# ScalarE's order in the second product's steps, the end of the routing, eight weight loads from another queue, and a branch made short

## The chip, the cores and the metric

The kernel runs on one core of one Trainium2 chip, as one program. The engines of the core run their own instruction streams and meet at semaphores: TensorE (PE in the profile, its weight loads PEld), VectorE (DVE), ScalarE (ACT), GpSimd (POOL) and SyncE (SP, which here only issues DMAs). The metric is the device time of one execution in microseconds. Three runs of the kernel before took 572.85, 573.92 and 575.16 us, median 573.92.

## The reference

Three parts follow each other, on 1536 tokens of width 512:

```python
# attention, 2 x 8 heads, 768 positions, head size 64
keep = is_global | is_local              # 8 global keys, 96 local ones
scores = np.where(keep, scale * q @ k.T - slope * dist, -1e9)
x = softmax(scores) @ v
# gated product
xn = x / rms(x) * rms_g
x = (silu(xn @ w_gate) * (xn @ w_val)) @ w_out        # d_ff 1536
# top-1 mixture of 8 experts; tokens with a skip score <= 0 are passed on
do = x @ w_skip > 0
e = argmax(x[do] @ w_gate_moe)           # 8 logits
y = prob[e] * (relu(x[do] @ w1[e]) @ w2[e])           # 512 -> 1024 -> 512
out = x;  out[do] = x[do] + y
```

## The kernel before

Numbers of full precision are needed, so each large matrix product is done as three: every operand is cast to a high part (names with h: `wh`, `hh`, `ewh`, `exh`) by ACT, and the rest (`wl`, `hl`, `ewl`, `exl`) is a subtraction on DVE or POOL. The order of the instructions on each engine is the order in which the code is written (a manual schedule), so a hook inside a loop places work by hand. Each engine works its own list off in order.

- **Start.** SP issues the loads; DVE works out a flag (are the attention's two limits in the range that the fast code handles?). `with tc.If(flag == 0): general_attention(s)` (L962) holds a general attention, which these inputs don't take: every engine branches over it. Its six query blocks are written out, inside a loop over head pairs.
- **Banded attention**, 24 items: scores (L222), maximum (L233), exponential (L244), product with v.
- **First product** `gemm1` (L517): gate and value, results `h` kept in SBUF, 18 tiles.
- **Second product** `gemm2(t)` (L583), twelve steps, one for 128 tokens each: 36 matmuls `px` of 128x512, ACT scales them out as `x2` (L587), a DMA of it goes to `out` from ACT's queue (L590) and another to a copy `xm` from SP's. Inside the loop over the twelve blocks k of a step stand hooks: `turn(t-1)` behind k=1 transposes the last step's x2 (L559, `pxt`) and ACT copies it to `x2t` (L560); `logits(t-1)` and `route(t-1)` behind k=4 compute the router's logits (L568, `lg`), on DVE the choice of an expert, and `exps` on ACT the exponential (`rex`, L656); `slots` behind k=9. Ahead of a step stand `ranks(t-2)` (L678/L679, `rk`): counts of tokens by expert. Behind a step, `split_h(t+2)` casts the operand of a later step in six pieces (ACT `hh` L546, DVE `hl` L547), and in the steps 1, 2, 5 and 6 `split_next` casts 3, 2, 2 and 1 tiles of the experts' weights (ACT `ewh` L824, DVE `ewl` L833, 128x1024 each).
- **Routing's end.** Each expert takes 128 token slots. Expert 0's tokens aren't gathered from DRAM but built on PE in `x0` by products with a selection matrix (`add`, L1180), for the last three steps by hand: `choose` makes the matrix from the rank `rk0` of the last tokens. While expert 0's first product runs, a hook `gathers` works out the token indices (`ids`, `gi_s`) and POOL gathers the tokens of experts 1, 0, 2, 3 by indirect DMAs (L848).
- **Experts** 0 to 8 (the ninth takes what didn't fit): `tx` transposes and splits the tokens (L858, L861), `up` (L871, `eph`), `relu`, `th` transposes and splits again (L890 to L893), `down` (L903, `epy`), `put` (L911 `eo`, and an indirect DMA to `out` from POOL, L913). Weight tiles of 512 KB come by 72 loads from SP (L816) into a ring of tiles (`eraw`), each split by ACT and DVE into two more tiles; a load waits until a tile is free, and its place in SP's list is where `load_next` is called.

Of the kernel before, what the change touches and what calls it, by code (L numbers as in the profile page):

```python
# [113 lines left out]
def general_attention(s):  # L114

    nc, tc = s.nc, s.tc
    with tc.tile_pool(name="ga", bufs=1) as p, tc.tile_pool(name="gap", bufs=1, space=PSUM) as ps:
        slopes = p.tile([128, 8, 2], F32, name="gslopes")
        for j in range(16):
            nc.gpsimd.memset(slopes[:, j // 2, j % 2:j % 2 + 1], -(2.0 ** -(j % 8 + 1)))  # L120
        with tc.For_i(0, 8, 1) as pr:
            slope = p.tile([128, 2], F32, name="gslope")
            nc.vector.tensor_copy(slope, slopes[:, ds(pr, 1), :].rearrange("p a b -> p (a b)"))
            for hh in range(2):
                r = slice(64 * hh, 64 * hh + 64)
                q = p.tile([64, 768], F32, name="gq")
                nc.sync.dma_start(q.rearrange("p (a i c) -> p a i c", a=1, c=64),
                                  s.qx.rearrange("a p (i c) -> p a i c", c=128)[r, ds(pr, 1), :, r])
                k = p.tile([64, 928], F32, name="gk")
                nc.sync.dma_start(k.rearrange("p (a n) -> p a n", a=1),  # L130
                                  s.kx.rearrange("a p n -> p a n")[r, ds(pr, 1), :])
                v = p.tile([128, 11, 64], F32, name="gv")
                nc.sync.dma_start(v.rearrange("p (a b) d -> p a b d", a=1),
                                  s.vx.rearrange("a p h b d -> p a h b d")[:, ds(pr, 1), hh])
                nc.vector.tensor_scalar(q, q, 0.125, None, ALU.mult)
                xo = p.tile([64, 768], F32, name="gxo")
                for i in range(6):
                    rel = p.tile([128, 768], F32, name="grel")
                    nc.gpsimd.iota(rel, pattern=[[-1, 768]], base=128 * i, channel_multiplier=1,
                                   allow_small_or_imprecise_dtypes=True)  # L140
                    key = p.tile([128, 768], F32, name="gkey")
                    nc.gpsimd.iota(key, pattern=[[1, 768]], base=0, channel_multiplier=0,
                                   allow_small_or_imprecise_dtypes=True)
                    loc = p.tile([128, 768], F32, name="gloc")
                    dist, keep = distance(s, rel, key, loc)
                    sc = ps.tile([128, 6, 128], F32, name="gsc")
                    for j in range(6):
                        nc.tensor.matmul(sc[:, j, :], lhsT=q[:, 128 * i:128 * i + 128],
                                         rhs=k[:, 160 * j:160 * j + 128], start=True, stop=True)
                    t = p.tile([128, 768], F32, name="gt")  # L150
                    nc.vector.scalar_tensor_tensor(
                        out=t, in0=dist, scalar=slope[:, hh:hh + 1], in1=sc.rearrange("p a b -> p (a b)"),
                        op0=ALU.mult, op1=ALU.add)
                    nc.vector.tensor_tensor(t, t, keep, ALU.mult)
                    nc.vector.tensor_scalar(keep, keep, 1.0, -NEG, ALU.subtract, ALU.mult)
                    nc.vector.tensor_tensor(t, t, keep, ALU.add)
                    m = p.tile([128, 1], F32, name="gm")
                    nc.vector.tensor_reduce(m, t, AX.X, ALU.max)
                    nc.vector.tensor_scalar(t, t, m, None, ALU.subtract)
                    z = p.tile([128, 1], F32, name="gz")  # L160
                    nc.scalar.activation(t, t, AF.Exp, accum_out=z)
                    nc.vector.tensor_scalar(z, z, 1e-9, None, ALU.add)
                    nc.vector.reciprocal(z, z)
                    nc.vector.tensor_scalar(t, t, z, None, ALU.mult)
                    pt = ps.tile([128, 6, 128], F32, name="gpt")
                    for j in range(6):
                        nc.tensor.transpose(pt[:, j, :], t[:, 128 * j:128 * j + 128], s.ident)
                    pts = loc.rearrange("p (a b) -> p a b", a=6)
                    nc.vector.tensor_copy(pts, pt)
                    po = ps.tile([64, 128], F32, name="gpo")  # L170
                    for j in range(6):
                        nc.tensor.matmul(po, lhsT=v[:, 2 * j, :], rhs=pts[:, j, :],
                                         start=j == 0, stop=j == 5)
                    nc.vector.tensor_copy(xo[:, 128 * i:128 * i + 128], po)
# [451 lines left out]

def route(s, t):

    V, p = s.nc.vector, s.hpool
# [169 lines left out]
class Expert:  # L799
# [52 lines left out]

    def tx(self, xt=None):
        s, nc = self.s, self.s.nc
        if xt is None:
            xt = s.ps_e.tile([128, 4, 128], F32, name="ext", bufs=1)
            for k in range(4):
                nc.tensor.transpose(xt[:, k, :], self.xg[:, 128 * k:128 * k + 128], s.ident)  # L858
        self.xh = s.epool.tile([128, 4, 128], F32R, name="exh", bufs=2)
        self.xl = s.epool.tile([128, 4, 128], F32R, name="exl", bufs=2)  # L860
        nc.scalar.copy(self.xh, xt)  # L861
        nc.vector.tensor_tensor(self.xl, xt, f(self.xh), ALU.subtract)

    def up(self, hook=None):
# [54 lines left out]
def attn_moe_kernel(ctx, tc, qx, kx, vx, rel, ints, wgv, w_out, rms_g, w9, w9t, w1, w2, out):  # L919
# [216 lines left out]
    def routed(t):  # L1136
        logits(s, t)
        run(route(s, t))
        exps(s, t)

    for t in range(11):
        if t >= 2:
            ranks(s, t - 2)
            run(select(s, t - 2))
        if t >= 2:
            run(gates(s, t - 2))
        gemm2(s, t, {
            (0, 1): lambda: t >= 1 and turn(s, t - 1),
            (0, 4): lambda: t >= 1 and routed(t - 1),
            (0, 9): lambda: t >= 2 and slots(s, t - 2)})  # L1150
        if t + 2 < 12:
            split_h(s, t + 2)
        if t in (1, 5, 9):
            for q in range(6):
                s.slots.add(early if t < 9 and q == 0 else big, [f"h{t // 4}{q}"])
        split_next({1: 3, 2: 2, 5: 2, 6: 1}.get(t, 0))
        load_next({6: 4, 9: 5}.get(t, 0))


    slt = s.ixpool.tile([24, 256], F32, name="slt", bufs=1)  # L1160
# [36 lines left out]
    def tenth():  # L1197
        ranks(s, 10)
        choose(10, s.rk[10], s.oh[:, 10, 0:1])

    def adds():
        add(s.x2[9], first[9], start=True)
        add(s.early, s.ident)
        free_wo(0, 3)
        load_next(4)

    gemm2(s, 11, {
        (0, 2): lambda: turn(s, 10), (0, 5): early, (0, 9): lambda: routed(10),
        (256, 4): lambda: turn(s, 11, 0), (256, 6): tenth, (256, 10): adds})
    logits(s, 11, range(2))  # L1210
    add(s.x2[10], first[10])
    turn(s, 11, 1)
    logits(s, 11, range(2, 4))
    lg = s.lg[11]
    nc.scalar.dma_start(s.out[1408:1536, :], s.x2[11])
    rest = route(s, 11)
# [4 lines left out]
                                   op0=ALU.is_equal, op1=ALU.mult)  # L1221
    rk0 = s.ps_g.tile([128, 1], F32, name="rk0", tag="ps0", bufs=2)
    nc.tensor.matmul(rk0, lhsT=s.ones16, rhs=s.cum[:, 11, 0:1], start=True, stop=False)
    nc.tensor.matmul(rk0, lhsT=s.tri, rhs=oh0, start=False, stop=True)
    choose(11, rk0, oh0)
    run(rest)
    exps(s, 11)
    add(s.x2[11], first[11], stop=True)
    free_wo(3, 6)
    ranks(s, 11, s.ps_m, "misc")  # L1230
    psr.close()
    hctx.close()
    gctx.close()
# [3 lines left out]
    s.slots.add(s.epool, ["raw8"])  # L1237
    s.ps_e = pool(phase3, "ps_e", space=PSUM)
    experts[0].tx(x0)
    run(select(s, 10), select(s, 11))  # L1240

    def gathers():
        p = ids(s.ps_m, "misc", False)
# [6 lines left out]
        for e in (1, 0, 2, 3):  # L1250
            experts[e].gather()

    experts[0].up(gathers)
    run(gates(s, 10), gates(s, 11))
    experts[0].relu()
    for t in range(9, 12):
        slots(s, t)
    slt2 = s.ixpool.tile([24, 256], F32, name="slt2", bufs=1)
    nc.vector.tensor_tensor(slt2, slt, s.sl, ALU.add)
    experts[1].tx()  # L1260
    experts[0].th()
    tab = s.ps_m.tile([128, 2, 24], F32, name="tab", tag="misc", bufs=1)
    for b in range(2):
        nc.tensor.transpose(tab[:, b, :], slt2[:, 128 * b:128 * b + 128], s.ident[0:24, 0:24])
# [125 lines left out]
```

## Time and profile before

| | us |
|---|---|
| median of three runs | 573.92 |
| the profiled execution | 574.41 |
| its span | 572.7 |
| attention | about 12 to 105 |
| first product | 105 to 310 |
| second product's steps | 310 to 439 |
| routing's end, to expert 0's first matmul | 439 to 445 |
| experts | 445 to 566 |

PE is busy 93% of the span, DVE 70%, ACT 48%, POOL 24%. In the second product the step's length is read from one rank product (`rk`) to the next; a timeline row gives start, duration, engine, line, operation, and in brackets the idle time of that engine before it with what ended it. [...]

### The profile page before, as it was taken

Reading aid. Unit: us, or ns where it says so; the run is one execution under the profiler, and the core shown is the slowest. Engines: PE = TensorE matmul, PEld = TensorE weight load, DVE = VectorE, ACT = ScalarE, POOL = GpSimd, SP = SyncE. Lnnn points to the kernel's source line nnn. Section 1 sums busy time; section 2 is a strip of 40 time slices with the busy share of each in tenths; the row PEclk is TensorE's granted clock in tenths of the full one; section 3 lists DMA queues with packets and bytes.
Section 4 is the critical chain, followed back from the end, with each engine's and each line's share of the span. In section 5 each row is a group of like instructions: output and inputs, shape, how many; then the busy total and the mean of one; then the engine's idle time right before and its main releaser. Section 6 shows DMA issues by size and latency. Waiting matters only on the chain. (4 is left out here: it accounts for less than half of the span.)

```text
span 572.7 us, 8709 instructions
## 1 busy us (share of the span) xinstructions
PE 532.6 (93%) x2932; PEld 444.9 (78%) x2932; DVE 401.0 (70%) x1014; ACT 277.7 (48%) x630; POOL 135.0 (24%) x132
## 2 busy tenths in 40 slices
PE   1899998899999999999999988989998799999994
PEld 1788887788888888888888867867888587878883
DVE  2888989557888688768864255545442299999971
ACT  0689889224323333323323444335231196988850
POOL 1445556011222222222212000000000201566201
PEclk9899999899999999999999988999999899999998
DMA  8645521021223323333206211106066899999000
GB/s 300 263 180 223 196 89 39 1 75 61 96 102 110 111 80 105 110 112 110 102 10 224 106 41 66 42 37 221 37 251 220 266 340 330 367 396 367 32 15 17
DMA packets 29511, 83.79 MB, mean 146 GB/s; under 512 B 3512, under 2 KB 3640, under 8 KB 29457
## 3 DMA queue, kind: packets, MB, share of 16 engines
q1 hardware_dynamic: 26064, 75.95, 36.7%
q0 software_dynamic: 1520, 4.03, 2.1%
q10 hardware_dynamic: 1872, 3.15, 1.5%
q8 instruction: 26, 0.43, 0.3%
q14 instruction: 29, 0.23, 0.1%
HBM read 75.42 MB, written 8.65 MB: 147 GB/s over the span
## 5 line engine op out<-in xcount | busy, mean ns | idle before, releaser
L517 PE MATMUL ps<-xh,wh 128*128 128x512 f32 (+1 forms) x304 | 115.9, 381 | 0.1
L517 PE MATMUL ps<-xh,wl 128*128 128x512 f32 (+1 forms) x304 | 115.3, 379 | 0.4 <-POOL wl L483 0.4
L517 PE MATMUL ps<-xl,wh 128*128 128x512 f32 (+1 forms) x304 | 115.2, 379 | 0.0
L833 DVE TENSOR_TENSOR ewl<-eraw,ewh 128x1024 fp32r<-128x1024 f32 x72 | 83.7, 1231 | 1.9 <-ACT ewh L824 1.7
L824 ACT CAST ewh<-eraw 128x1024 fp32r<-128x1024 f32 x72 | 71.3, 1057 | 7.0 <-DVE ewl L833 6.7
L517 PEld LDWEIGHTS ps<-xh,wl 128*128 128x128 f32 x304 | 57.3, 189 | 11.7 <-POOL wl L483 0.9
L517 PEld LDWEIGHTS ps<-xh,wh 128*128 128x128 f32 x304 | 57.4, 189 | 11.2 <-issue 0.8
L517 PEld LDWEIGHTS ps<-xl,wh 128*128 128x128 f32 x304 | 57.5, 189 | 10.6
L470 DVE SCALAR_TENSOR_TENSOR wraw<-f64t,wraw 128x512 f32<-128x512 f32 x36 | 44.0, 1221 | 28.8 <-ACT f64t L468 28.8
L583 PE MATMUL px<-woh,hh 128*128 128x512 f32 (+1 forms) x156 | 62.8, 403 | 0.0
L547 DVE TENSOR_TENSOR hl<-h,hh 128x256 fp32r<-128x256 f32 x72 | 25.5, 423 | 50.7 <-ACT hh L546 50.7
L583 PE MATMUL px<-wol,hh 128*128 128x512 f32 (+1 forms) x156 | 59.7, 383 | 0.0
L583 PE MATMUL px<-woh,hl 128*128 128x512 f32 (+1 forms) x156 | 59.6, 382 | 0.0
L483 POOL TENSOR_TENSOR wl<-f64t,wh 128x512 fp32r<-128x512 f32 x24 | 31.0, 1292 | 101.4 <-ACT wh L482 58.1
L222 PE MATMUL sc<-kd,qd 128*128 128x192 f32 (+1 forms) x192 | 39.0, 353 | 12.3 <-DVEq L962 12.3
L244 ACT ACTIVATE es<-es,m 128x192 f32<-128x192 f32 (+1 forms) x96 | 41.5, 435 | 17.3 <-DVE m L233 16.3
L482 ACT CAST wh<-f64t 128x512 fp32r<-128x512 f32 x24 | 14.9, 621 | 71.4 <-DVE f64t L480 71.4
L260 POOL TENSOR_SCALAR es<-es,z 128x192 f32<-128x192 f32 x46 | 35.6, 784 | 43.6 <-DVE z L253 17.4
L222 PEld LDWEIGHTS sc<-kd,qd 128*128 128x128 f32 x192 | 32.9, 211 | 15.2 <-PEq L962 12.3
L583 PEld LDWEIGHTS px<-woh,hl 128*128 128x128 f32 x156 | 30.2, 193 | 5.8
L583 PEld LDWEIGHTS px<-woh,hh 128*128 128x128 f32 x156 | 30.1, 193 | 5.3
L583 PEld LDWEIGHTS px<-wol,hh 128*128 128x128 f32 x156 | 30.2, 194 | 4.2
(192 smaller groups left out, 974.2 us busy)
## 6 DMA issues: line engine op xcount, KB each, us to landing
eraw<-in_w_dram SPq DMA_DIRECT2D x72, 512.0 KB, 6.5
wraw<-in_wgv_dram SPq DMA_DIRECT2D x24, 512.0 KB, 3.7
wraw<-in_w_out_dram SPq DMA_DIRECT2D x12, 512.0 KB, 3.2
vp<-in_vx_dram SPq DMA_DIRECT2D x8, 704.0 KB, 5.0
qd<-in_qx_dram SPq DMA_DIRECT2D x7, 768.0 KB, 5.6
kd<-in_kx_dram SPq DMA_DIRECT2D x7, 464.0 KB, 6.6
xm<-x SPq DMA_DIRECT2D x12, 256.0 KB, 2.6
out_dram<-x ACTq DMA_DIRECT2D x12, 256.0 KB, 2.9
```

The lines of the kernel that those rows point to most:

```text
L222: nc.tensor.matmul(sc[r][:, x, 0:n], lhsT=qs[pr][:, 2 * (2 * g + r) + x, :], rhs=ks[pr][:, k0:k0 + n], start=True, stop=True)
L244: nc.scalar.activation(e[:, r, x, e0:e0 + n], e[:, r, x, e0:e0 + n], AF.Exp, bias=m[:, j:j + 1], scale=-1.0, accum_out=z[:, j:j + 1])
L260: eng.tensor_scalar(e[:, r, x, e0:e0 + n], e[:, r, x, e0:e0 + n], z[:, j:j + 1], None, ALU.mult)
L470: nc.vector.scalar_tensor_tensor(out=a.bitcast(F32), in0=t, scalar=F64_LEAST, in1=a.bitcast(F32), op0=ALU.is_ge, op1=ALU.mult)
L482: nc.scalar.copy(hi, t)
L483: eng.tensor_tensor(lo, t, f(hi), ALU.subtract)
L517: nc.tensor.matmul(p, lhsT=w[:, k, :], rhs=x[c][:, k, a:b], start=n == 0, stop=n == 11)
L547: nc.vector.tensor_tensor(hl[:, i, :], src, f(hh[:, i, :]), ALU.subtract)
L583: nc.tensor.matmul(p, lhsT=h[:, k, :], rhs=w[k][:, c:c + N], start=n == 0, stop=n == 35)
L824: eng.copy(wh, raw)
L833: eng.tensor_tensor(wl, raw, f(wh), ALU.subtract)
```

## The change

1. `general_attention`: the six query blocks become a loop, `tc.For_i(0, 6, 1)`. The code isn't executed with these inputs, it becomes shorter: in the built program the branch goes over 120 instructions on DVE (before 267), 107 on PE (before 255), 70 on ACT (before 46) and 88 on POOL (before 64), loop control and semaphores included, a matmul and its weight load counted as one.
2. Second product's steps: `split_h` for a step stands behind `turn` in the hook of the step before it, in place of one step earlier behind the matmuls; `logits`, `route` and `exps` move from behind k=4 to behind k=5; the weight casts follow them (in steps 2, 3, 6 and 7) in place of standing behind steps 1, 2, 5 and 6. Some weight loads move with them.
3. Routing's end: `keep(n)` puts eight matmuls on PE whose result nobody reads (`idle`), the second transposition moves ahead of the products with x2[10], the exponentials and ranks of the last step go behind expert 0's `tx`, whose high cast is done in two halves.
4. Behind the four gathers POOL issues eight of the experts' weight loads; SP goes on with those that follow. Expert 0's `th` stands ahead of expert 1's `tx`.

```diff
@@ general_attention
-                for i in range(6):
+                rel0 = p.tile([128, 768], F32, name="grel0")
+                nc.gpsimd.iota(rel0, pattern=[[-1, 768]], base=0, channel_multiplier=1,
+                               allow_small_or_imprecise_dtypes=True)
...
+                with tc.For_i(0, 6, 1) as i:
...
+                    nc.vector.tensor_copy(rel, rel0)
...
+                    nc.vector.tensor_scalar(rel0, rel0, 128.0, None, ALU.add)
@@ Expert.tx
-        nc.scalar.copy(self.xh, xt)
+        for k in ((0, 2), (2, 4)) if x0 else ((0, 4),):
+            nc.scalar.copy(self.xh[:, k[0]:k[1], :], xt[:, k[0]:k[1], :])
@@ steps of the second product
-        gemm2(s, t, {
-            (0, 1): lambda: t >= 1 and turn(s, t - 1),
-            (0, 4): lambda: t >= 1 and routed(t - 1),
-            (0, 9): lambda: t >= 2 and slots(s, t - 2)})
-        if t + 2 < 12:
-            split_h(s, t + 2)
...
-        split_next({1: 3, 2: 2, 5: 2, 6: 1}.get(t, 0))
-        load_next({6: 4, 9: 5}.get(t, 0))
+        def one():
+            if t >= 1:
+                turn(s, t - 1)
+                split_h(s, t + 1)
...
+                load_next({6: 0, 10: 6}.get(t, 0))
+        def two():
+            if t >= 1:
+                routed(t - 1)
+            split_next({2: 3, 3: 2, 6: 2, 7: 1}.get(t, 0))
+            load_next({7: 4}.get(t, 0))
+        gemm2(s, t, {(0, 1): one, (0, 5): two, (0, 9): lambda: t >= 2 and slots(s, t - 2)})
@@ routing's end
-        load_next(4)
+    def keep(n):
+        w = experts[0].w[0][0]
+        for _ in range(n):
+            nc.tensor.matmul(idle, lhsT=w[:, 0:128], rhs=w[:, 512:1024], start=True, stop=True)
...
-    add(s.x2[10], first[10])
+    keep(1)
     turn(s, 11, 1)
+    add(s.x2[10], first[10], range(2))
     logits(s, 11, range(2, 4))
+    add(s.x2[10], first[10], range(2, 4))
...
+    keep(2)
     nc.tensor.matmul(rk0, lhsT=s.tri, rhs=oh0, start=False, stop=True)
     choose(11, rk0, oh0)
+    keep(2)
+    add(s.x2[11], first[11], stop=True)
+    keep(3)
     run(rest)
-    exps(s, 11)
-    add(s.x2[11], first[11], stop=True)
...
     experts[0].tx(x0)
-    run(select(s, 10), select(s, 11))
+    exps(s, 11)
+    ranks(s, 11, s.ps_m, "misc")
+    run(select(s, 11))
...
             experts[e].gather()
+        load_next(8, nc.gpsimd)
...
+    experts[0].th()
     experts[1].tx()
-    experts[0].th()
```

ACT's list in a step with three weight casts, from the evacuation of a step's result to the next one, before:

```order
L587 ACTIVATE x_3904<-px,r_1722 128x512
L590 DMA out_dram<-x_3904 128x512
L546 CAST hh<-h_795 128x256
L546 CAST hh<-h_2356 128x256
L546 CAST hh<-h_2357 128x256
L546 CAST hh<-h_2358 128x256
L546 CAST hh<-h_2359 128x256
L546 CAST hh<-h_2360 128x256
L824 CAST ewh<-eraw 128x1024 x3
L560 COPY x2t<-pxt 128x512
L656 ACTIVATE rex,rz<-lg,rm 128x8
```

and in the changed kernel:

```order
L596 ACTIVATE x_3456<-px,r_1288 128x512
L599 DMA out_dram<-x_3456 128x512
L569 COPY x2t<-pxt 128x512
L555 CAST hh<-h_361 128x256
L555 CAST hh<-h_1922 128x256
L555 CAST hh<-h_1923 128x256
L555 CAST hh<-h_1924 128x256
L555 CAST hh<-h_1925 128x256
L555 CAST hh<-h_1926 128x256
L665 ACTIVATE rex,rz<-lg,rm 128x8
L833 CAST ewh<-eraw 128x1024 x3
```

The copy x2t moved from behind nine casts to right behind the evacuation; the weight casts moved from ahead of it to the end, behind the exponential.

PE's list at the end of the routing, from the last step's last matmul to the first of expert 0 (`x` is x0, written by `add`; `sel` a selection matrix), before:

```order
L583 MATMUL px<-woh_2349,hl 128x256
L568 MATMUL lg<-w9t,x2t 128x9 x2
L1180 MATMUL x_4898<-sel_5022,x_4827 128x128 x4
L559 MATMUL pxt<-ident,x_4915 128x128 x2
L568 MATMUL lg<-w9t,x2t 128x9 x2
L1223 LDWEIGHTS ones_3824
L1223 MATMUL rk_5077<-cum,ones_3824 128x1
L1224 LDWEIGHTS tri
L1224 MATMUL rk_5077<-oh_5075,tri 128x1
L1180 MATMUL x_4898<-sel_5080,x_4915 128x128 x4
```

and in the changed kernel:

```order
L577 MATMUL lg<-w9t,x2t 128x9 x2
L1228 MATMUL idle<-ewh 128x512
L568 MATMUL pxt<-ident,x_4483 128x128 x2
L1197 MATMUL x_4466<-sel_4590,x_4369 128x128 x2
L577 MATMUL lg<-w9t,x2t 128x9 x2
L1197 MATMUL x_4466<-sel_4590,x_4369 128x128 x2
L1249 LDWEIGHTS ones_3390
L1249 MATMUL rk_4650<-cum,ones_3390 128x1
L1228 MATMUL idle<-ewh 128x512 x2
L1251 LDWEIGHTS tri
L1251 MATMUL rk_4650<-oh_4648,tri 128x1
L1228 MATMUL idle<-ewh 128x512 x2
```

The transposition moved ahead of the four products with x2[10], two of which now stand on each side of the last logits; the unread matmuls stand ahead of each instruction that waits for another engine (three more follow the products with x2[11], which are next in both lists).

## Rows read from the trace of the kernel before

**Rows 1.** The page: TensorE's busy time (the first of the engines on its line) and the two queues of instruction fetches (packets, MB, share).

```profile
PE 532.6 (93%) x2932; PEld 444.9 (78%) x2932; DVE 401.0 (70%) x1014; ACT 277.7 (48%) x630; POOL 135.0 (24%) x132
...
q8 instruction: 26, 0.43, 0.3%
q14 instruction: 29, 0.23, 0.1%
```

**Rows 2.** Busy time of the engines in two stretches of 30 us: the stretch, its length, the busy time of each engine with its instructions, PEclk, DMA share, GB/s.

```profile
0.00:30.00 30.00, 15.45 (x86) 14.02 (x88) 16.36 (x76) 12.12 (x46) 8.20 (x23) 0.94 0.77 287
...
480.00:510.00 30.00, 29.70 (x147) 24.37 (x146) 30.00 (x32) 25.66 (x34) 15.55 (x5) 1.00 0.97 357
```

**Rows 3.** The instructions of line 962, the branch over the general attention: engine (q: its sequencer), operation, count, duration in ns (least, median, longest), start of the first and last. POOL's semaphore event stands behind its branch.

```profile
L962 PEldq COMPARE_BRANCH  x1: 6047/6047/6047, 5.7 to 5.7; - x1
...
L962 POOLq EVENT_SEMAPHORE  x1: 17/17/17, 6.1 to 6.1; - x1
```

**Rows 4.** The timeline of DVE: the first instruction behind the branch.

```profile
12.32 0.37 DVE L104 TENSOR_SCALAR keep<-rel,gl 128x576 f16<-128x576 f16 x1 [7.28 <-DVEq L962]
```

**Rows 5.** The first queries and keys: the first two issues of the queries' load, then the time from issue to landing (least, median, longest) of the four loads of queries and of the four of keys issued in the first 20 us.

```profile
L202 SPq DMA_DIRECT2D qd<-in_qx_dram x2: 423/428/432, 1.7 to 2.7; - x2
...
DMA to landing us min/median/max: 4.0/7.0/13.4
...
DMA to landing us min/median/max: 3.9/7.6/14.1
```

**Rows 6.** Stretches: steps of the second product from one rk to the next, with TensorE alone (stretch, length, PE's busy time, PEclk, DMA share, GB/s); then with all engines (as rows 2) the time behind the first step's wait and the beginning of expert 0.

```profile
327.64:341.79 14.15, 11.71 (x54) 0.88 0.10 39
341.79:355.01 13.22, 11.73 (x54) 0.87 0.10 40
374.73:386.35 11.62, 10.13 (x53) 1.00 0.12 46
386.35:397.06 10.71, 10.16 (x54) 1.00 0.71 247
355.01:364.86 9.85, 9.85 (x54) 1.00 0.14 53
...
336.00:340.00 4.00, 4.00 (x13) 3.17 (x12) 1.87 (x13) 0.36 (x2) 0.00 (x0) 0.64 0.00 0
...
444.70:448.10 3.40, 2.91 (x7) 1.88 (x7) 1.61 (x7) 0.44 (x1) 0.00 (x0) 0.50 0.47 155
```

**Rows 7.** The waits of TensorE from 326 to 440 us: in total, times, longest.

```profile
PE lg L568 <- ACT x2t L560: 6.0, 4, 2.4
```

**Rows 8.** The timeline of ACT in the step from 327.67 on, and TensorE's transposes for x2t in it.

```profile
327.80 0.69 ACT L587 ACTIVATE x<-px,r 128x512 f32<-128x512 f32 x1 [1.81 <-PE rk L679]
...
328.92 1.94 ACT L546 CAST hh<-h 128x256 fp32r<-128x256 f32 x6 [0.43 <-ACT x L587]
330.76 2.94 ACT L824 CAST ewh<-eraw 128x1024 fp32r<-128x1024 f32 x3
333.60 0.57 ACT L560 COPY x2t<-pxt 128x512 f32<-128x512 f32 x1
...
329.13 0.60 PE L559 MATMUL pxt<-ident,x 128*128 128x128 f32 x4
```

**Rows 9.** The timeline of TensorE from the last matmul of the second product into the experts.

```profile
439.17 0.28 PE L583 MATMUL px<-woh,hl 128*128 128x256 f32 x1
...
445.19 1.22 PE L871 MATMUL eph<-ewh,exh 128*128 128x512 f32 x2 [0.73 <-ACT exh L861]
...
448.05 0.40 PE L1167 MATMUL ids<-ident,slt 8*128 8x8 f32 x2
...
448.73 0.71 PE L871 MATMUL eph<-ewh,exh 128*128 128x512 f32 x2
...
452.96 0.51 PE L699 MATMUL sl<-sel,val 128*24 128x256 f32 x3
456.67 0.63 PE L858 MATMUL ext<-ident,exg 128*128 128x128 f32 x4 [3.20 <-DMA exg<-xm,gi_s]
...
458.33 0.73 PE L871 MATMUL eph<-ewh,exh 128*128 128x512 f32 x2
...
478.09 0.47 PE L903 MATMUL epy<-ewh,ehh 128*128 128x512 f32 x1 [1.11 <-DVE eo L911]
```

**Rows 10.** The timeline of POOL: the first gather, and one beside DVE's weight subtractions; then the landing of the gather `early` of the second product's last step, and the page's row of the weight loads (KB each, median from issue to landing).

```profile
449.85 1.00 POOL L848 DMA_INDIRECT exg<-xm,gi_s  x1 [17.47 <-DVE rz L665]
...
491.08 6.17 POOL L848 DMA_INDIRECT exg<-xm,gi_s  x1 [0.30 <-PE ext L858]
...
DMA to landing us min/median/max: 3.4/3.4/3.4
...
eraw<-in_w_dram SPq DMA_DIRECT2D x72, 512.0 KB, 6.5
```

**Rows 11.** The timeline of DVE behind expert 0's first product, and of ACT where the weights of the 25th and 26th load are cast.

```profile
460.07 9.17 DVE L833 TENSOR_TENSOR ewl<-eraw,ewh 128x1024 fp32r<-128x1024 f32 x8
...
473.79 3.50 DVE L833 TENSOR_TENSOR ewl<-eraw,ewh 128x1024 fp32r<-128x1024 f32 x3
477.20 0.75 DVE L911 SCALAR_TENSOR_TENSOR eo<-epy,gate,exg 128x512 f32<-128x512 f32 x1
...
481.61 2.02 ACT L824 CAST ewh<-eraw 128x1024 fp32r<-128x1024 f32 x2
```

More of the change, by code (lines that the diff above doesn't have):

```diff
@@ L134, in general_attention @@
                                   s.vx.rearrange("a p h b d -> p a h b d")[:, ds(pr, 1), hh])
-                nc.vector.tensor_scalar(q, q, 0.125, None, ALU.mult)
                 xo = p.tile([64, 768], F32, name="gxo")
-                for i in range(6):
+                rel0 = p.tile([128, 768], F32, name="grel0")
+                nc.gpsimd.iota(rel0, pattern=[[-1, 768]], base=0, channel_multiplier=1,
+                               allow_small_or_imprecise_dtypes=True)
+                key0 = p.tile([128, 768], F32, name="gkey0")
+                nc.gpsimd.iota(key0, pattern=[[1, 768]], base=0, channel_multiplier=0,
+                               allow_small_or_imprecise_dtypes=True)
+                with tc.For_i(0, 6, 1) as i:
+                    qi = p.tile([64, 128], F32, name="gqi")
+                    nc.vector.tensor_scalar(qi.rearrange("p (a c) -> p a c", a=1),
+                                            q.rearrange("p (i c) -> p i c", c=128)[:, ds(i, 1), :],
+                                            0.125, None, ALU.mult)
                     rel = p.tile([128, 768], F32, name="grel")
-                    nc.gpsimd.iota(rel, pattern=[[-1, 768]], base=128 * i, channel_multiplier=1,
-                                   allow_small_or_imprecise_dtypes=True)
+                    nc.vector.tensor_copy(rel, rel0)
                     key = p.tile([128, 768], F32, name="gkey")
-                    nc.gpsimd.iota(key, pattern=[[1, 768]], base=0, channel_multiplier=0,
-                                   allow_small_or_imprecise_dtypes=True)
+                    nc.vector.tensor_copy(key, key0)
                     loc = p.tile([128, 768], F32, name="gloc")
@@ L147, in general_attention @@
                     for j in range(6):
-                        nc.tensor.matmul(sc[:, j, :], lhsT=q[:, 128 * i:128 * i + 128],
-                                         rhs=k[:, 160 * j:160 * j + 128], start=True, stop=True)
+                        nc.tensor.matmul(sc[:, j, :], lhsT=qi, rhs=k[:, 160 * j:160 * j + 128],
+                                         start=True, stop=True)
                     t = p.tile([128, 768], F32, name="gt")
@@ L173, in general_attention @@
                                          start=j == 0, stop=j == 5)
-                    nc.vector.tensor_copy(xo[:, 128 * i:128 * i + 128], po)
+                    nc.vector.tensor_copy(xo.rearrange("p (i c) -> p i c", c=128)[:, ds(i, 1), :],
+                                          po.rearrange("p (a c) -> p a c", a=1))
+                    nc.vector.tensor_scalar(rel0, rel0, 128.0, None, ALU.add)
                 nc.sync.dma_start(s.xg.rearrange("(a h p) n -> p a h n", h=2, p=64)[:, ds(pr, 1), hh, :],
@@ L627, in route @@
 def route(s, t):
-    V, p = s.nc.vector, s.hpool
+    V, p = s.nc.vector, s.ixpool if t == 11 else s.hpool
     lg, skip = s.lg[t][:, 0:8], s.lg[t][:, 8:9]
@@ L854, in tx @@
         s, nc = self.s, self.s.nc
-        if xt is None:
+        x0 = xt is not None
+        if not x0:
             xt = s.ps_e.tile([128, 4, 128], F32, name="ext", bufs=1)
@@ L1146, in attn_moe_kernel @@
             run(gates(s, t - 2))
-        gemm2(s, t, {
-            (0, 1): lambda: t >= 1 and turn(s, t - 1),
-            (0, 4): lambda: t >= 1 and routed(t - 1),
-            (0, 9): lambda: t >= 2 and slots(s, t - 2)})
-        if t + 2 < 12:
-            split_h(s, t + 2)
-        if t in (1, 5, 9):
-            for q in range(6):
-                s.slots.add(early if t < 9 and q == 0 else big, [f"h{t // 4}{q}"])
-        split_next({1: 3, 2: 2, 5: 2, 6: 1}.get(t, 0))
-        load_next({6: 4, 9: 5}.get(t, 0))
+        def one():
+            if t >= 1:
+                turn(s, t - 1)
+                split_h(s, t + 1)
+            if t in (2, 6, 10):
+                for q in range(6):
+                    s.slots.add(early if t < 10 and q == 0 else big, [f"h{t // 4}{q}"])
+                load_next({6: 0, 10: 6}.get(t, 0))
[5 more added lines that the diff above has]
+        gemm2(s, t, {(0, 1): one, (0, 5): two, (0, 9): lambda: t >= 2 and slots(s, t - 2)})
     slt = s.ixpool.tile([24, 256], F32, name="slt", bufs=1)
@@ L1199, in tenth @@
         choose(10, s.rk[10], s.oh[:, 10, 0:1])
+        run(select(s, 10), gates(s, 10))
     def adds():
@@ L1209, in attn_moe_kernel @@
         (256, 4): lambda: turn(s, 11, 0), (256, 6): tenth, (256, 10): adds})
+    idle = s.ps_m.tile([128, 512], F32, name="idle", tag="misc", bufs=1)
     logits(s, 11, range(2))
-    add(s.x2[10], first[10])
+    keep(1)
     turn(s, 11, 1)
+    add(s.x2[10], first[10], range(2))
     logits(s, 11, range(2, 4))
+    add(s.x2[10], first[10], range(2, 4))
     lg = s.lg[11]
@@ L1223, in attn_moe_kernel @@
     nc.tensor.matmul(rk0, lhsT=s.ones16, rhs=s.cum[:, 11, 0:1], start=True, stop=False)
+    keep(2)
     nc.tensor.matmul(rk0, lhsT=s.tri, rhs=oh0, start=False, stop=True)
     choose(11, rk0, oh0)
+    keep(2)
+    add(s.x2[11], first[11], stop=True)
+    keep(3)
     run(rest)
-    exps(s, 11)
-    add(s.x2[11], first[11], stop=True)
     free_wo(3, 6)
-    ranks(s, 11, s.ps_m, "misc")
     psr.close()
@@ L1251, in gathers @@
             experts[e].gather()
+        load_next(8, nc.gpsimd)
     experts[0].up(gathers)
-    run(gates(s, 10), gates(s, 11))
+    run(gates(s, 11))
     experts[0].relu()
@@ L1257, in attn_moe_kernel @@
         slots(s, t)
-    slt2 = s.ixpool.tile([24, 256], F32, name="slt2", bufs=1)
+    slt2 = s.ixpool.tile([24, 256], F32, name="slt2", tag="early", bufs=1)
     nc.vector.tensor_tensor(slt2, slt, s.sl, ALU.add)
+    experts[0].th()
     experts[1].tx()
-    experts[0].th()
     tab = s.ps_m.tile([128, 2, 24], F32, name="tab", tag="misc", bufs=1)
```

## The prediction

> **What bounds the kernel now.** I read the page's first two parts first. TensorE (PE) is busy 93% of the 572.7 us span and VectorE (DVE) 70%, ScalarE (ACT) and GpSimd (POOL) less [rows 1]: time can only go where PE is idle or runs at a low clock, or where another engine holds it back. So I looked for PE's idle time stage by stage: 14.6 us in the first 30 us, 0.3 us in the 30 us from 480 on [rows 2], 6.0 us of waits in the second product's steps [rows 7], 3.2 us in one wait of the routing's end [rows 9]. The reader should see these three holes, one for each region that the diff touches, and a full PE elsewhere. The wait views say what ended each. The median of the runs shown is 573.92 us; the profiled execution took 574.41 us, of which 572.7 are span. I make the sum against 574.41 and take off the 0.49 at the end.
>
> **Start (general attention in a loop).** That code isn't executed with these inputs: all engines branch over it at L962. POOL's branch, over 64 instructions in the built program, lets it go on at 6.1 us. DVE's goes over 267 and PE's over 255 (those of PE nearly all matmuls, each with its weight load as a second instruction); PE's branch lasts 6.05 us from 5.7 on [rows 3], and DVE's first work starts at 12.32, released by "DVEq L962" [rows 4]. So a far branch cost some 6.1 us and a near one at most 0.4. Nothing else holds that work back: the first queries, issued at 1.7 us, land at the earliest 4.0 us later, and the keys, issued next, take 3.9 [rows 5], so both are there by about 6.1; what DVE's first instruction reads was issued before them. In the changed program the branch goes over 120 instructions on DVE, 107 on PE, 70 on ACT and 88 on POOL. Nothing in the trace shows a branch over 120, or PE's over 107 with its weight loads, some 215. The instruction fetches come in packets of 0.23 MB / 29 = 8 KB on one queue and 0.43 MB / 26 = 17 KB on the other [rows 1]. All of them over the 8709 instructions of the page are 0.66 MB / 8709 = 76 bytes, a little less if branches and semaphore events are counted too: a packet holds at least 105 or 218 instructions. So 64 ahead hits, 267 (and PE's 510 with weight loads) misses, and 120 and 215 lie about one packet ahead. Bounds: 0 (still a miss) and 6.2 us (resume at 6.1). I take -6.1, since what is one packet ahead should be there by the time of a branch 5.7 us into the program. The stage behind it follows its start one for one, as DVE's items come one after the other; what could be late instead is a load of the next heads: the latest lands 14.1 us after its issue [rows 5], near 20 us, and belongs to the third pair, whose turn on DVE comes at 9.3 + 4 x 3.9 = 24.9 (24 items in the 93 us of attention).
>
> [...]
>
> **The second product's steps.** Between two ranks matmuls (rk) a step without a weight cast lasts 9.85 us, the four with casts 14.15, 13.22, 11.62 and 10.71 [rows 6]: 4.30 + 3.37 + 1.77 + 0.86 = 10.3 us over. [...] Why x2t is late stands in ACT's rows: x at 327.80, six hh casts (1.94), three ewh casts (2.94), and only then x2t at 333.60, though its transposes were done at 329.73 [rows 8]. In the new order x2t follows x and its out DMA directly: counted from the step's start, x is done at 0.9 us, the transposes end at 2.1, x2t at 2.7, and the logits stand behind the sixth of twelve blocks, at 4.5 or later. Then hh, 1.94 us, to 4.7 (its reader is the next step, 5 us off); the exponential waits for the DVE's maximum and runs near 7; then at most three ewh casts, 2.94, to 10.0, which is 0.1 us into the next step, where x waits for it by at most 0.2 us and has until that step's transposes, 1.5 us in. DVE's ewl for the last cast ends 1.3 us later still; behind it wait only the hl of the next step but one. So no new PE wait is visible, and I take nearly the whole: -10.2 us; bounds -6 (the clock falls all the same and only the idle returns) and -10.3.
>
> **Routing's end.** Before: last px at 439.17, up-matmuls (eph) of expert 0 from 445.19 behind waits of up to 0.73 us [rows 9], in a stretch at clock 0.50 [rows 6]: the first six take 445.19 to 448.05 = 2.86 us, the later ones, from 448.73 on with the clock back, start 0.24 us apart (two at 448.73, the 18 of them by 452.96), which is 1.4 for six. The filler of 8 unread matmuls of about 0.24 us lies in the waits; where it is longer than its wait it delays, by 0.2 us in all. The exponential leaves ACT's way before exh, and exh in halves lets the first up matmul start 0.3 us earlier: eph at 444.7. With the clock held the six take 1.4: -1.4. ids, indices and POOL's first gather, at 449.85 before [rows 10], follow at 449.85 - 0.5 - 1.4 = 447.9. The gather took 6.8 us to be landed (449.85 to 456.67), amid weight loads that SP issued; the early one took 3.4 [rows 10]. Now SP issues none there before the gathers, and POOL's stand behind them; I take 5.0, the middle: landed at 452.9. Before, 456.67 + 1.66 to up(1) at 458.33; now th (1.0 us PE) lies ahead of tx, in the wait: 452.9 + 1.35 = 454.2. What then sets the time is DVE: its ewl chain starts at 460.07, and eo (477.20), which down(1) at 478.09 waits for, ends a chain of work that fills DVE, 18.0 us behind that start [rows 9, 11]. The chain may start behind ehl, exl and tabs, 455.1 by the same shifts: -5.0. Behind 478, PE is the bound (0.3 us idle in 30 [rows 2]), so the shift reaches the end. Bounds: -2.0 (landing 6.8 us, clock not held) and -6.
>
> **POOL's eight weight loads.** Each needs POOL to issue it. Nothing in the trace shows a plain load from POOL; the nearest rows are gathers: 1.0 us when DVE is quiet, 6.17 us from 491.08 on, when DVE runs ewl back to back [rows 10]. The loads start at about 453, two of them before DVE's chain. Load number 26, the last of POOL's, was cast at 482.6 before, the second of two [rows 11], now at 477.6; with 6.5 us of landing [rows 10] POOL must have issued all eight by 471, so up to (471 - 453)/8 = 2.2 us each costs nothing. I take 1.0 to 1.6: nothing lost. Upper bound, six loads at 6.47 each: issued by 494.4, 23 us late.
>
> [...]
>
> Sum: -6.1 - 10.2 - 5.0 = -21.3; 574.4 - 21.3 = 553.1, less 0.49: 552.6, forecast 553. What is not touched (first product, experts 2 to 8) I cost at nothing.
>
> **Rivals.** (a) The branch still misses on DVE or PE: the other two terms stay, 553 + 6.1 = 559. For it: nothing shown between 64 and 255. Against: the packet sizes [rows 1]. (b) The waits go but the clock falls all the same behind some other pause, and the gather lands as before: 10.2 becomes 6 to 8, 5.0 becomes 2 to 3: 553 + 5 = 558. Against: the steps without a wait, or with a short one, have clock 1.00 [rows 6]. (c) POOL's loads are blocked by DVE's streaks until the streak ends. DVE's first streak lasts 9.2 us and the one after the small job instructions 3.5 [rows 11]: loads 3 to 6 leave after 464, 7 and 8 after 472.5, so the last lands about 3 us late: up to 556, and 560 where landing takes 4 us more in the crowd. (d) The other side: each load blocks by itself for 6 us and more, as each gather does, and down(1) and up(3) wait for weights while the out scatter and later gathers queue behind the loads on POOL. From (471 + 21.3 - 453)/8 = 4.9 us a load the gain is gone; at the bound, 553 + 23 = 576, slower than before. Against: a stalled cast leaves DVE idle, and then POOL goes on.
>
> **Chances.** Forecast with its own range 549.5 to 556: 0.55. (a) 0.18, (b) 0.08, (c) 0.14, (d) with what else could lose everything 0.05. The range holds 549.5 to 561.5, all cases but the last and some sums of two. Within 0.5% of 573.92 (571.1 to 576.8, about what a measurement of this kernel tells from no change): only (d) reaches it. Faster 0.93, same 0.03, slower 0.04.
>
> **What would show it.** Start: DVE's first work after the branch at about 6.3 us, not 12.3. Steps: no "lg waits for ACT x2t", every step 9.85 to 9.9 us, clock 1.00 from 310 to 440. Routing: eph about 5.5 us after the last px and at full clock, first gather about 8.7 us after the last px (10.7 before), ewl's chain 16 us (20.9 before). POOL: eight loads of 1 to 2 us each; if they show 6 us, (c) or (d) holds, and PE waits for ewh or ewl in up(2), down(1) or up(3). The prediction is wrong if the steps keep a wait, if DVE resumes after 10 us, or if PE waits for weights behind 460.

## The result and the profile after

The changed kernel took 554.55 us in the median of four runs (553.78 to 556.02), the kernel before 574.33: a ratio of 0.966, 95% interval 0.9645 to 0.9682, faster by 19.8 us. The forecast was 553.0 us in a range of 549.5 to 561.5. The profiled span fell from 572.7 to 552.9 us.

Where it went is read from five marks that both traces have, one profile of each kernel (us from the span's start):

| mark | before | after | moved by | in this stage | forecast |
|---|---|---|---|---|---|
| DVE's first work behind the branch | 12.32 | 6.38 | -5.94 | -5.94 | -6.1 |
| first px (the second product starts) | 309.83 | 303.17 | -6.66 | -0.72 | 0 |
| last px (its last matmul) | 439.17 | 422.67 | -16.50 | -9.84 | -10.2 |
| first matmul of down(1) | 478.09 | 457.26 | -20.83 | -4.33 | -5.0 |
| end | 572.7 | 552.9 | -19.8 | +1.0 | 0 |

**Start.** Line 973 is now the branch, as line 962 in [rows 3]; behind it DVE's first work, as in [rows 4]:

```profile
L973 PEldq COMPARE_BRANCH  x1: 233/233/233, 5.6 to 5.6; - x1
...
6.38 1.08 DVE L104 TENSOR_SCALAR keep<-rel,gl 128x576 f16<-128x576 f16 x1 [1.37 <-DVEq L973]
```

PE's branch lasts 0.23 us in place of 6.05, DVE resumes 0.7 us after its own.

**Steps.** The four steps of [rows 6], the one without a cast, and the microseconds 336 to 340, which had a granted clock (PEclk, a share of TensorE's full speed) of 0.64 there (first TensorE alone, then all engines):

```profile
321.02:330.92 9.90, 9.90 (x55) 1.00 0.14 54
330.92:340.83 9.91, 9.91 (x55) 1.00 0.15 55
360.62:370.53 9.91, 9.91 (x55) 1.00 0.14 53
370.53:380.43 9.90, 9.90 (x55) 1.00 0.61 213
340.83:350.71 9.88, 9.88 (x55) 1.00 0.14 53
...
336.00:340.00 4.00, 4.00 (x21) 3.31 (x21) 2.37 (x11) 2.05 (x4) 0.00 (x0) 1.00 0.00 2
```

PE is busy for the whole of each, and every step takes 9.9 us, with weight casts or without. The view of waits has no row left for TensorE between 303 and 425 us, where [rows 7] stood, and the granted clock is 1.00 from 303 to 427. ACT's timeline of the first such step, as [rows 8]:

```profile
321.13 0.69 ACT L596 ACTIVATE x<-px,r 128x512 f32<-128x512 f32 x1 [1.14 <-PE rk L688]
...
323.14 0.59 ACT L569 COPY x2t<-pxt 128x512 f32<-128x512 f32 x1 [1.33 <-PE pxt L568]
323.62 1.94 ACT L555 CAST hh<-h 128x256 fp32r<-128x256 f32 x6
328.04 0.27 ACT L665 ACTIVATE rex<-lg,rm 128x8 f32<-128x8 f32 x1 [2.48 <-DVE rm L662]
...
328.30 2.93 ACT L833 CAST ewh<-eraw 128x1024 fp32r<-128x1024 f32 x3
```

x2t is done 2.7 us into the step, and the casts run at its end, where nobody waits for them; ACT idles for 2.48 us ahead of the exponential.

**Routing's end**, TensorE as in [rows 9], and the granted clock where expert 0 starts, beside 0.50 in [rows 6]:

```profile
422.67 0.29 PE L592 MATMUL px<-woh,hl 128*128 128x256 f32 x1
...
428.61 0.71 PE L882 MATMUL eph<-ewh,exh 128*128 128x512 f32 x2
...
430.18 0.38 PE L1184 MATMUL ids<-ident,slt 8*128 8x8 f32 x2
...
436.72 0.61 PE L868 MATMUL ext<-ident,exg 128*128 128x128 f32 x4
...
438.23 0.73 PE L882 MATMUL eph<-ewh,exh 128*128 128x512 f32 x2 [0.67 <-ACT exh L872]
```

```profile
427.90:431.30 3.40, 3.34 (x18) 2.38 (x17) 1.57 (x8) 0.95 (x4) 0.00 (x0) 1.00 0.00 0
```

Expert 0 starts 5.94 us behind the last px (6.02 before); its first six matmuls take 430.18 - 428.61 = 1.57 us in place of 2.86; `ext` no longer waits for the gather. POOL, as in [rows 10], and DVE's chain, as in [rows 11]:

```profile
431.96 1.00 POOL L857 DMA_INDIRECT exg<-xm,gi_s  x1 [16.07 <-DVE rz L674]
...
436.87 3.16 POOL L825 DMA_DIRECT2D eraw<-in_w_dram  x5
440.68 0.53 POOL L825 DMA_DIRECT2D eraw<-in_w_dram  x1 [0.65 <-DMA exg<-xm,gi_s]
442.40 0.72 POOL L825 DMA_DIRECT2D eraw<-in_w_dram  x1 [1.18 <-DMA exg<-xm,gi_s]
444.14 0.72 POOL L825 DMA_DIRECT2D eraw<-in_w_dram  x1 [1.03 <-DMA exg<-xm,gi_s]
...
470.26 6.16 POOL L857 DMA_INDIRECT exg<-xm,gi_s  x1 [0.30 <-issue]
```

```profile
439.24 9.17 DVE L842 TENSOR_TENSOR ewl<-eraw,ewh 128x1024 fp32r<-128x1024 f32 x8
...
456.37 0.74 DVE L922 SCALAR_TENSOR_TENSOR eo<-epy,gate,exg 128x512 f32<-128x512 f32 x1
```

A weight load keeps POOL for 0.5 to 0.7 us, also the three inside DVE's unbroken 9.17 us of ewl, while a gather beside such a stretch still takes 6.16. All eight loads are issued by 444.9 us.

**Experts**, TensorE's wait ahead of down(3), before:

```profile
502.97 0.63 PE L858 MATMUL ext<-ident,exg 128*128 128x128 f32 x4 [0.30 <-DMA exg<-xm,gi_s]
```

and after:

```profile
482.50 0.63 PE L868 MATMUL ext<-ident,exg 128*128 128x128 f32 x4 [0.42 <-issue]
```

### The profile page after: what moved, and what is told of

Read it like the earlier page. It is cut to its first block, busy times and chain, and to the rows that moved or that the text cites. A ratio compares the mean times of both kernels' runs of the same rounds, so it can differ in the third digit from the quotient of the medians.

```text
span 552.9 us, 8722 instructions
## 1 busy us (share of the span) xinstructions
PE 528.6 (96%) x2940; PEld 440.9 (80%) x2940; DVE 403.4 (73%) x1014; ACT 277.6 (50%) x631; POOL 140.3 (25%) x140
## 5 line engine op out<-in xcount | busy, mean ns | idle before, releaser
L592 PE MATMUL px<-wol,hh 128*128 128x512 f32 (+1 forms) x156 | 58.2, 373 | 0.0
L231 PE MATMUL sc<-kd,qd 128*128 128x192 f32 (+1 forms) x192 | 36.8, 339 | 6.4 <-DVEq L973 6.4
L231 PEld LDWEIGHTS sc<-kd,qd 128*128 128x128 f32 x192 | 30.7, 200 | 9.3 <-PEq L973 6.4
```

Source lines behind the costliest of these rows:

```text
L231: nc.tensor.matmul(sc[r][:, x, 0:n], lhsT=qs[pr][:, 2 * (2 * g + r) + x, :], rhs=ks[pr][:, k0:k0 + n], start=True, stop=True)
L592: nc.tensor.matmul(p, lhsT=h[:, k, :], rhs=w[k][:, c:c + N], start=n == 0, stop=n == 35)
```

## The experiments

Times are medians; the kernel before took 573.9 to 574.6 us beside them. Marks are taken from the profiles.

**e1_unrolled**: the loop alone undone.

```diff
-                with tc.For_i(0, 6, 1) as i:
+                for i in range(6):
```

> The changed kernel with general attention written out again (the branch goes over 267 instructions on DVE and 255 on PE), all else as changed. Theory, the length of the branch decides the start: DVE's first work behind the branch at about 12.3 us in place of 6.4, the first product starts 6 us later, and the time is 554.55 + 5.9 to 6.7 = 560.5 to 561.3 us. Rival, the start came earlier for another reason (loads, other code at the start): within 1 us of 554.55.

Measured: 559.99 us (558.21 to 561.03), 5.4 over the changed kernel, half a microsecond less than the theory's least. PE's branch takes 5.94 us, DVE's first work comes at 12.84, 6.5 us later. The first px came only 4.0 us later than in the changed kernel; this one profile has no stretch at half clock in the attention (last section), which fits, but was not tried.

**e2_loop_alone**: the kernel before with the loop as the only edit.

> The kernel before with the loop in general attention alone. Theory, the start's gain stands by itself and reaches the end: DVE at 6.4 us, time 574.33 - 5.9 to 6.7 = 567.6 to 568.4 us, and the steps of the second product keep their waits of 6.0 us. Rival, later stages take it back (weights that land no earlier, DMAs of the attention that crowd each other): 571 us or more.

Measured: 570.06 us (566.44 to 571.01), ratio 0.991 (0.9875 to 0.9947). DVE's first work at 6.48, first px at 303.11, 6.72 earlier. The steps keep their four waits; in this profile the half clock behind the first lasted from 327.4 to 334.2 and that step 15.72 us in place of 14.15, and a wait of 1.49 us came up at 499. So the start's gain reaches the second product whole, and some 3 us of it were lost again behind it in this profile, a run of 570.63. The median, 4.2 us below the kernel before, lies between theory and rival; two of the five runs took 566.44 and 567.37, a little less than the theory says, and no profile shows those.

**e8_far**: 80 memsets of a small tile on DVE, in the code that is jumped over.

```diff
+        pad = p.tile([128, 2], F32, name="gpad")
+        for _ in range(80):
+            nc.vector.memset(pad, 0.0)
         with tc.For_i(0, 8, 1) as pr:
```

> The changed kernel with 80 more small memsets on DVE in the code that the branch jumps over (they aren't executed): DVE's branch goes over 200 instructions in place of 120, the other engines' as before. Theory A, a target is there only if it lies about one packet of fetched instructions (105 to 128) ahead: DVE's first work at about 12 us, PE's first at 6.4 as now or waiting with it, 560.5 us. Theory B, the packet behind that one is there too: DVE at 6.4 us and 554.6 us.

Measured: 559.22 us (two runs). The branch of PE (0.23 us) and DVE's first work:

```profile
L976 PEldq COMPARE_BRANCH  x1: 233/233/233, 5.8 to 5.8; - x1
...
11.73 0.37 DVE L104 TENSOR_SCALAR keep<-rel,gl 128x576 f16<-128x576 f16 x1 [6.58 <-DVEq L976]
```

Of the two, theory A holds: 120 instructions ahead are there, 200 are not. PE's first work waits for DVE here, until 11.72 us, though its own branch took 0.23. That the limit is a packet is not shown, and no run gives the 128 of theory A (the 105 is an estimate from [rows 1]): the runs place the limit between 120 and 200 on DVE.

**e3_old_steps**: the steps' order of before in the changed kernel (its loop of steps put back, one more weight load in step 9).

> The changed kernel with the old order in the second product's steps (transposes behind block 1, logits behind block 4, split_h two steps ahead and the weight casts behind the steps 1, 2, 5 and 6), the weight loads in number as in the changed kernel. Theory, the order of ACT's list made the gain of the steps: four waits of lg for x2t, 6.0 us together, steps of about 14.1, 13.2, 11.6 and 10.7 us, the clock at 0.50 behind the two longest, and 554.55 + 9.8 = 564.4 us. Rival, the clock's part came from elsewhere: only the waits return, 560.5 us.

Measured: 566.84 us (565.93 to 567.98). TensorE's steps and waits:

```profile
322.52:336.64 14.12, 11.70 (x54) 0.88 0.10 38
336.64:349.86 13.22, 11.74 (x54) 0.87 0.11 41
369.65:381.30 11.65, 10.17 (x54) 1.00 0.12 45
381.30:391.98 10.68, 10.15 (x54) 1.00 0.73 246
```

```profile
PE lg L577 <- ACT x2t L569: 5.9, 4, 2.4
```

The old steps within 0.03 us each, clock included: from the first px to the first of the last half step it is 123.2 us in place of 113.2. Of the other 2 us of its median 1.5 lie ahead of the steps in the profile, with the first px at 304.69 (last section).

**e7_casts_first**: x2t first as changed, but the weight casts right behind hh, ahead of the logits.

```diff
                 split_h(s, t + 1)
...
+            split_next({2: 3, 3: 2, 6: 2, 7: 1}.get(t, 0))
...
                 routed(t - 1)
-            split_next({2: 3, 3: 2, 6: 2, 7: 1}.get(t, 0))
```

> The changed kernel with the weight casts of the second product's steps right behind the six hh casts, ahead of logits and exponential (they stay in the same steps, behind x2t). Theory, only the place of x2t ahead of the casts matters: no wait, steps of 9.9 us, 554.6 to 555.7 us. Rival, the exponential, its sum and the next evacuation come late behind the casts and TensorE or DVE waits: steps over 10 us, 557 us or more.

Measured: 554.16 us (553.9 to 555.59), no wait of TensorE in the steps. What counts is x2t's place; where the casts stand behind it is free. That `logits` moved by a block was not tried alone, but in the changed kernel x2t is done 2.7 us into the step, and the block behind which `logits` stood before ends at 4.0.

**after_again**, **e4_no_filler**, **e6_fewer**: the changed kernel, and with none and with six of the eight unread matmuls.

```diff
-    keep(1)
...
-    keep(2)
...
-    keep(2)
...
-    keep(3)
```

> The changed kernel itself, as the mark for the three kernels beside it: 554.5 us, DVE's first work at 6.4 us, steps of 9.9 us, first matmul of expert 0 5.9 us behind the last px, first gather 9.3 behind it, DVE's ewl chain 16.6 behind it. Stretches at half clock in the attention, where they stand in other places than at 95.5 to 98.9 us, tell what one of them costs.

> The changed kernel without the eight unread matmuls. Theory, they hold the clock and cost some time themselves: the first matmul of expert 0 comes 0.5 to 0.7 us earlier (5.3 us behind the last px), the clock is 0.50 from there for 3.4 us, the first six matmuls take 2.86 us in place of 1.57, the gather comes 0.6 to 0.8 us later, and the time is 555.2 us. Rival, the other order of the routing has left too little idle time for the clock to fall: 1.00 throughout, everything 0.6 us earlier, 553.9 us.

> The changed kernel with six unread matmuls in place of eight (one less ahead of the rank product that waits for DVE, one less ahead of expert 0). Theory, each of the two runs on past the end of its wait and delays the chain: the first matmul of expert 0 comes 0.4 to 0.5 us earlier with the clock at 1.00, 554.1 us. Rival, the clock falls again: 555.4 us.

Measured: 555.68 (554.16 to 555.91), 553.57 (552.62 to 554.55) and 555.5 us (553.4 to 556.01); ratios to before 0.966, 0.964 and 0.9655, with intervals that overlap. So the times settle nothing: the first is 1.2 us above its expectation, and the third has the rival's time (555.4). The first px comes at 304.63, 302.67 and 304.73, ahead of everything that these edits touch. The marks behind it tell them apart: the first matmul of expert 0 comes 5.93, 5.18 and 5.48 us behind the last px, down(1) 34.58, 33.95 and 34.16. Without any filler:

```profile
427.35 0.74 PE L882 MATMUL eph<-ewh,exh 128*128 128x512 f32 x2 [0.43 <-ACT exh L872]
```

```profile
427.30:430.70 3.40, 3.35 (x16) 2.47 (x17) 2.07 (x11) 0.63 (x3) 0.00 (x0) 1.00 0.00 0
```

The clock stays at 1.00 all the same, and with six fillers the first two matmuls of expert 0 take 0.71 us, as with eight (1.22 in [rows 9], at 0.50): e4's rival is right, and the fillers only cost, 0.75 us at expert 0 and 0.63 at down(1).

**e12_old_routing**: no fillers, and the old order at the routing's end.

```diff
-    turn(s, 11, 1)
-    add(s.x2[10], first[10], range(2))
+    add(s.x2[10], first[10])
+    turn(s, 11, 1)
     logits(s, 11, range(2, 4))
-    add(s.x2[10], first[10], range(2, 4))
...
+    exps(s, 11)
     add(s.x2[11], first[11], stop=True)
```

> The changed kernel without the unread matmuls and with the old order at the routing's end (products with x2[10] ahead of the second transposition, the last exponential and its minus ahead of expert 0's high cast). Theory, it is this order that held the clock, since it leaves less idle time between the last px and expert 0: waits of 0.5 us each as before return, the clock falls to 0.50 near expert 0's first matmuls, which take 2.9 us for six, and down(1) comes some 2 us later than without the fillers: 555.5 us. Rival, the full clock of the steps ahead of it holds it: 1.00 and 554.2 us.

Measured: 555.32 us (554.99 to 557.85), down(1) 35.79 us behind the last px, 1.84 later than without fillers. Four waits of 0.46, 0.56, 0.45 and 0.52 us are back within 4 us (e4 has 0.22, 0.45 and 0.43), and with them the fall of the clock:

```profile
428.60 1.22 PE L882 MATMUL eph<-ewh,exh 128*128 128x512 f32 x2 [0.52 <-ACT exh L872]
```

```profile
428.10:431.50 3.40, 2.90 (x7) 1.87 (x7) 1.28 (x4) 0.72 (x4) 0.00 (x0) 0.50 0.00 0
```

So it is the order that holds the clock: with the old one it falls at expert 0's start in all three profiles (before, e2, e12), with the new one in none of the eleven. That it does so by the idle time it takes away is read from these waits.

**e5_loads_sp**: the eight loads given back to SP.

```diff
-        load_next(8, nc.gpsimd)
+        load_next(8)
```

> The changed kernel with POOL's eight weight loads given back to SP. Theory, SP's loads then run beside the gathers as in the kernel before: the first gather takes 6.8 us or more to land in place of at most 4.8, TensorE waits some 2 us for it, and DVE's ewl chain starts 1.5 to 2 us later: 556.3 us. Rival, the gather is covered by th, which stands ahead of it now, and four of SP's loads run beside it anyway: 554.5 us.

Measured: 556.83 us (555.8 to 557.34), 1.15 over the changed kernel beside it; the intervals of their ratios overlap, and the marks decide.

```profile
431.39 1.00 POOL L857 DMA_INDIRECT exg<-xm,gi_s  x1 [16.08 <-DVE rz L674]
```

```profile
438.00 0.66 PE L868 MATMUL ext<-ident,exg 128*128 128x128 f32 x4 [1.70 <-DMA exg<-xm,gi_s]
```

The gather is landed 6.6 us after its issue, in place of 4.8 at most, TensorE waits 1.70 us, the clock falls once more (440.3 to 443.7; two matmuls of `up` take 1.05 us there, 0.63 before it), and down(1) comes 37.3 us behind the last px, 2.75 later; from there to the end it is 94.6 us, 0.6 to 1.0 less than in the two profiles of the changed kernel.

**e13_tx_first**: `tx` of expert 1 ahead of `th` of expert 0.

```diff
-    experts[0].th()
     experts[1].tx()
+    experts[0].th()
```

> The changed kernel with expert 1's tx ahead of expert 0's th, as in the kernel before. Theory of the prediction, th fills the wait for the first gather: TensorE waits for the gather again, by the 1.0 us that th's eight transposes took of it, ACT's two casts of th come behind exh, and DVE's ewl chain starts 0.5 to 1 us later: down(1) 35.1 to 35.6 us behind the last px in place of 34.6, 555.5 us. Rival, the gather is there before both and the order is free: down(1) at 34.6, the time of the changed kernel, 554.6 to 555.7 us.

Measured: 555.43 us (555.32 to 557.0), ratio 0.967. The time fits theory and rival alike. `ext` waits 1.44 us for a gather landed 5.0 us after its issue, and down(1) comes 35.80 us behind the last px, 1.22 later than in the changed kernel: the theory, a little above its range.

**e10_old_places**: no fillers, and the experts' tiles at the addresses of the kernel before.

```diff
-    V, p = s.nc.vector, s.ixpool if t == 11 else s.hpool
+    V, p = s.nc.vector, s.hpool
...
-    slt2 = s.ixpool.tile([24, 256], F32, name="slt2", tag="early", bufs=1)
+    slt2 = s.ixpool.tile([24, 256], F32, name="slt2", bufs=1)
```

> The changed kernel without the unread matmuls, and with two small tiles put back (slt2 in a place of its own, the last route's temporaries in their old pool), so that the experts' tiles lie at the same addresses in SBUF as in the kernel before; in the changed kernel they lie 832 bytes further. Theory, the places make the experts' matmuls start 0.229 us apart before and 0.2325 in every kernel built on the change: 0.229 again, the time from the first matmul of down(1) to the end 94.6 us in place of 95.3 to 95.6, total 552.5 us. Rival, something else in the change does it: 0.2325 and 553.6 us as without the fillers.

Measured: 552.98 us (552.14 to 553.62), ratio 0.9638 (0.9617 to 0.9659), the fastest median of all, but between theory and rival, and with an interval that overlaps e4's. What tells them apart is the pace of matmuls. The second and the last of the 24 matmuls of down(3), here and in e4:

```profile
482.15 0.39 PE L914 MATMUL epy<-ewl,ehh 128*128 128x512 f32 x1
...
487.20 0.39 PE L914 MATMUL epy<-ewh,ehl 128*128 128x512 f32 x1
```

```profile
481.46 0.40 PE L914 MATMUL epy<-ewl,ehh 128*128 128x512 f32 x1
...
486.55 0.40 PE L914 MATMUL epy<-ewh,ehl 128*128 128x512 f32 x1
```

5.05 / 22 = 0.2295 us apart in place of 5.09 / 22 = 0.2314; in the two kernels of the comparison it is 5.05 before and 5.09 after. Over all distances within a `down` (without the longest and shortest 5%) the mean is 0.2305 to 0.2308 in the three profiles with the old places (the kernel before, e2, e10) and 0.2326 to 0.2331 in the eleven with the new ones, whatever else they change. From the first matmul of down(1) to that of down(8) it is 80.8 us, in e4 81.3, neither with a wait ahead of down(3); the steps take 9.85 us again. From down(1) to the end it is 94.3 and 95.3, but 0.4 of this 1.0 lies behind the last matmul, where the fourteen profiles differ by as much (7.6 to 8.3 us).

## Why the prediction was right

- **Start**: -6.1 forecast, -5.94 measured at DVE, and the time moved by 5.4 (e1) and 4.2 (e2). Distance decides (e8: DVE's first work at 11.73 us over 200 instructions, 6.38 over 120). Of what lies "about one packet ahead", 120 on DVE and PE's 215 are there, and 200 on DVE is not. That fits packets of 8 KB for DVE and 17 KB for PE, an estimate from [rows 1] at 76 bytes an instruction, but no row says which queue is whose. Rival (a) falls. A further 0.7 us came by the first px, where the forecast had none: the half clock that before ran from 103.4 to 106.8 us, into the first product (start 104.9), now ends with 98.9 where it begins. No edit tried it, but the profiles bear it out: the first product lasts 204.9 us before and 204.3 after, 204.1 in the four others with less than 0.1 us of such a stretch in it (e1, e2, e8, e10), and 205.1 and 205.2 with 2.1 and 2.4 us of it (e4, e12). It was luck of this profile: in after_again the first px moved by 5.2 us, 0.9 less than forecast.
- **Steps**: -10.2 forecast, -9.84 measured. By [rows 6] the four steps with casts are 10.3 us over: PE idles 6.0 of them, is busy 3.7 longer in the two with 0.88 and 0.87 of the clock, and 0.6 longer in the other two. Both parts, the waits and the clock behind the two longest, came back with e3 (5.9 us; 0.88 and 0.87) and only with the order. Rival (b) falls. The 0.4 us missing are 9.90 in place of 9.85 a step, which e10 gives back: the tiles' places, a term that the prediction did not have.
- **Routing's end**: -5.0 forecast, -4.33 measured, and its steps differ more than the sum. "By 0.2 us in all" for the fillers was the failed one: they cost 0.75 us (e4), so expert 0 started 0.08 us earlier and not 0.5. The first gather came 9.3 us behind the last px (8.7 forecast, 10.7 before), DVE's chain 16.6 (16 forecast, 20.9 before). "With the clock held the six take 1.4: -1.4" measured 1.57, -1.29; but the clock was held by the order (e12), not by the filler (e4). The gather landed within 4.8 us; where POOL has the loads and the trace shows the landing it took 4.7 to 5.0 (e1, e3, e8, e13). The 5.0 forecast was the middle of two rows, and in part luck: four loads of SP stand beside the gather in the trace, which "SP issues none there" had excluded. The eight loads given back to SP cost 1.7 us of waiting (e5). th filled the wait (e13).
- **POOL's loads**: 1.0 to 1.6 us each forecast, 0.5 to 0.7 measured. The 1.0 is a gather beside a quiet DVE [rows 10]; that a load takes little more beside ewl was the author's estimate, which no row of before showed. Rival (c), by which DVE's streaks hold the loads back, and (d), which took the gathers' 6.17 us as the price, fall: inside DVE's stretch of ewl a load took 0.53 to 0.72 us, beside a later one a gather 6.16. What makes the two differ no run shows.
- **Experts**, costed at nothing: +1.0. Half of it is the places of the tiles (e10), 832 bytes further because two small tiles lie in another pool. Another 0.3 lies between the starts of down(2) and down(3), where TensorE waits 0.42 us ahead of `ext` in place of 0.30, and 0.2 behind the last matmul; no edit tried these two, and both differ by as much among the eleven profiles with the new places (waits of 0 to 0.53). Why the places slow a matmul by 1% stays open: the tiles that px reads and writes lie at the same addresses in the programs of e4 and e10, and its steps differ all the same. The forecast's miss of 1.5 us is this 1.0, 0.4 in the steps and 0.7 at the routing's end, less 0.6 at the start.

## What to carry to other kernels

Look for the copy that PE waits for and put it first in its engine's list; casts that nobody waits for go behind it, and the idle time taken away brings back more than itself where the clock falls behind it (taking away 6.0 us of waits brought 9.8 here). Code that isn't run counts when a branch goes over it: keep it short (over 120 instructions DVE's first work came at 6.38 us here, over 200 at 11.73). Try a filler against none once the order is changed; here the order had made it useless.

## What was not expected

- The granted clock stands at 0.50 for 3.4 us in the attention, at places that differ between profiles: near its end (95 to 107 us) in all but e1, and near its beginning (18 to 28 us) in 8 of the 14. The changed kernel had no such stretch near 19 in one profile and 19.0 to 22.4 in the other, and its first px came at 303.17 and 304.63: some 1.4 us that have nothing to do with an edit. Of the kernels with the short branch, the six with the early stretch have their first px at 304.0 to 304.7, the five without at 302.6 to 303.3. That it makes most of the scatter of the runs is likely and not shown: few of them have a profile.
- Moving tiles by 832 bytes changed the pace of matmuls by up to 1%, 0.5 us in the experts and 0.5 in the steps.
- Without fillers and with the old places the kernel takes 552.98 us, against 555.68 and 554.55 of the changed one; the intervals of the ratios overlap, so only its marks, not its time, show it to be better.
